# Group 4's keys and queries of a packed attention loaded as whole rows and transposed by PE and ACT; one line of the planner's transfer times and the issue order made anew

## The chip, the cores and the metric

The kernel runs on one core of a Trainium2 chip. The metric is the device time of one execution in microseconds (us). A core has five engines with their own instruction queues: PE (matrix products, with PEld loading its weights), DVE (vector work), ACT (activations and copies), POOL and SP. SP here only issues DMA transfers, which run on the core's 16 DMA engines.

## The reference

A packed attention in two stages feeds a gated feed-forward block. All arrays are float32, except the weights of the block, which come as float64 and are narrowed on the chip.

```python
# batch 8, heads 8, seq 576, head_dim 64, 32 packing queries, d_model 512, d_ff 1024
def _attn_ref(q, k, v, p):
    scale = 1.0 / np.sqrt(q.shape[-1])
    def sm_attn(qq, kk, vv):
        s = scale * np.matmul(qq, kk.transpose(0, 1, 3, 2))
        s = s - np.max(s, axis=-1, keepdims=True)
        a = np.exp(s)
        a = a / (np.sum(a, axis=-1, keepdims=True) + 1e-09)
        return np.matmul(a, vv)
    p_packed = sm_attn(p, k, v)          # 32 rows per head
    return sm_attn(q, p_packed, p_packed)

def _moe_ref(x, w_in, conv_w, w_out):    # x: heads side by side
    h = np.maximum(x @ w_in, 0.0)
    ...                                  # conv_out: 3 taps along the sequence
    gate = 1.0 / (1.0 + np.exp(-conv_out))
    return (h * gate @ w_out)
```

## The kernel before

**Groups.** The 64 pairs of batch and head are worked in 16 groups of four heads, g = 0 to 15; a batch is two groups. For each group the kernel loads the keys and queries (`load_kq`), the values (`load_v`, two transfers) and, for four groups at once, the packing queries (`load_p`). Keys and queries must stand with the head dimension on the partitions, so each is transposed (`head_transpose`). `attention` then has PE multiply packing queries and keys (line 450), DVE take the row maximum (495), ACT take the exponential (499), PE transpose it (525, copied by ACT in 528; from g = 10 on DVE and small transfers do this, 507 to 518), PE multiply with the values (535), ACT divide (546), PE transpose (551) and ACT copy the packed rows (554). The second attention is one more score (450), a transpose on DVE (559), a softmax (563 to 578), a transpose (583) and a split in a high and a low part (587, 589).

**Two layouts of keys and queries.** `by_block(g)` (lines 356 and 357) says which is used. Where it holds, one transfer brings whole rows (line 394: 128 partitions of 1152 numbers), PE transposes them in nine 128x128 pieces (434) and ACT copies them out of PSUM in two pieces of 640 and 512 columns (440). Where it doesn't, four transfers bring 32-number pieces of rows (405), and DVE transposes in one instruction (417). `in_order` and `as_scored` follow the same switch for the order of the columns of the scores. Before, it holds for g below 4.

**The block.** Instead of making the attention's output, the kernel multiplies the packed rows with w_in (`packed_weight`, line 609; high part 621, low part 625 and 629 in batches 0 and 1, and 632 later), and multiplies the second attention's probabilities with that (`ffn1`, line 661: 12 products for each of 8 batches x 8 slices of d_ff). ReLU, the three taps and the gate follow on ACT (673, 677, 687) and DVE (679, 683, 689). `ffn2` splits the result (700, 703) and multiplies it with w_out (752, eight steps of three products for each of 36 tiles of 128 rows), copies (760) and stores (762). w_in and w_out come in eight loads of 1 MB (295); ACT and DVE narrow them (265, 267, 272); w_out is also split (323, 328, 332).

**The order.** Every piece of work is a stream of steps (a Python generator), and the string `ORDER` says which stream makes its next step; each engine gets its instructions in that order and works them strictly so. `Flow` follows the same steps with planned times. These times only decide one thing in the program: where the plan has PE idle, `warm` puts in products that nobody reads (line 244, called fillers below). `SLOW` stretches the planned time of a transfer that begins before a given time. PSUM holds three buffers `big`, one `sm` and one `fo`.

Of the kernel before, what the change touches and what calls it, by code (L numbers as in the profile page):

```python
# [18 lines left out]


ORDER = (
    "0002043m0408043u0304030305060b3l0c06013k050b060c0g0c0c0b060605053q3v3k0e06070e070a3k063v06063k0j060e3v09060j3s0k"
    "0f0j0o060k0e0f3n0k0i0h3r3r060k0d063k0e0m0d3k3r060d0r0e0e0d060e060e060m060e0m0r3t0m0m3t0s0r400e3w0w0s0e0s0n0z0e0e"
    "3t0s0l0e0n060z0z0l0l0e3y170e46460m0q060m0e0u0e0u0l0m460m0e41460p410m170m0e0m0u17480u3x493x480v410v0m0u3x48410m4a"
    "49484a10474849474a3z0m414948413z491f4a49124248470u0u4a4a474b124b0t490u124b0t14433z0u0t0m4a434b0m4c0t4d1f4b4b434c"
    "0u441f4d0x4c4b3z12120u4e18434e3z1a0u4c120m4d4c4g3o6e130u1a154c3z0u131a124c6e450m0u434e4d45126e0u4e434g4f0m456e4g"
    "1a0u1n0m0u124f6e1n451l4d4e4f6e0u454f4d1a4h1c4e4e0u0u4f4g1b0y1k4d451b4i4f4f114j4i7e1n7e4k4i6e1g4h6f4j6e6e4i6f6e4k"
    "4h4k4i4j4i7f161i121a4k4j4i6e1i6f6f121e1a4j4k4l7f1d126f6f6f6f4j4k4l1i6f1o4k6g121s4l1i4l6g4h124l7g4m1a4l6f1a1j4m1q"
    "191j1i1a6f4m4j121i6g1q7g1w6g6h6e4n6g4m6h1q204n1a1v6g1i6g4m1v4l1h6g4m1a4n124m121r1v4n6g6g236f7h1a6g4o121i4n1i4o4p"
    "6h6h4o4p4p1a236h124o7h4o6h4n1q6g4p1a6h6h6h4p6h4o1m4o1a1y4n234p4p1q1i6h1i1q4q282b1y4r6i1r1y6i1y1a1i6i126i6i1q1a2b"  # L30
    "4r6i12241a4q4q1z6i6j1a6i1a4r1i6i6i4s6i2b1p4s6j4s1q4t4u1q4s1i1y1i4t4s264t1t4t1q1z6k1y2g6j2c4u6j1y4u4s261i6j2j4u6j"
    "4s6k6j264u2j4v4t2j1q6j271i4u1u4v226i4u6j266j4t2e1x4w2k6j4t1i4v1q2e1i1q6k4w2e4v2a1i1q6h2f2e4v3p6k6k6k4w1y1i274x26"
    "6k1q6k6l1y4x6l216k6k6k2f4x1q6k4x2m1y4v50266m1q6l6l4w264v1q2r2m6l2h4w6l2m2r506l4x2r6l4y4w1q4y291y6l6l4w501q4y6l6m"
    "4z6m4z262o2n4x1q6m4z2e6m4y6m6m2z1y4x4z6m264y4y4z524z1y4y52524z6l6m251y522s6m34536n535354542e6m2m542e26512u526n6n"
    "6o6n546j6n261y516n532z54526n2z6n6n6n52541y376n516o376p5554553753536m6o262u6o2w552e5630266o6o55266o5635535655266o"
    "6o57552n5756551y56566o2i6p6o1y586p262u6p586q562e596p262d58596p6p6n596p2m6p1y586p6q58576p2m2e6o2u57595a1y5732592m"
    "6q2l1y58586q57266q596q6q3232572m3f2m6q362q6q592e266r6q5b6q262m6r3f2e265a5b6r6r6s6p6r6r5a5c2m6r6s2e5d6r6r5c2e6r5c"
    "5d2m5b5c5c5d5e6r2m6s2e5c6s5e325c5f2u2e5d5e5e6r5d5d383f5e5f2e6s5f5e336s6s6t2v5f6s6s2e6t5k3a2m5d2p2u6s5f5f6s5k5g6t"
    "5e2m3c5g3a2x6t5g2v6t5h2m6t2e6q2m6t2u6t6u2e325k2m6t6u5h2u6t5h6t5f5h5i5h6t3g5h2e5i6u2m5i6u2t2y6u6u5h6u5j333a3a6v5g"
    "6u5j2u6u6u5i5g5i5j326u6v2u3i5j2m5i5j5j5i6v6v6v2m5g5m2u6v6u5m5j5m2u5n6v2u5g325m6v3a6v6w5m6v3d5m3i6w5n5n6v5o5m6w6w"  # L40
    "32313i6w3b6x3i6w5n32325o3a5l5n5o6w3j5l6v5o6w6x32326w6w5o3b325n2u325p6w6x6y5n325l5p3j6x5q6s5o5o6x3a2u5r6x6x5p6x5p"
    "2u5q5q5r6x6x5r6y5p5p3a5q3i6x3e6z5r5p325s2u5q6x325q5s2u5r6y2u6y6y6y3a5q5s5t6z396y2u6y5r5r6y5t6y3a3i5u5t5s6y5t5s3a"
    "325s2u5t325t5s5u325v5t6z326z6z5u6z6w6z3i703i6z703i6z3a6z5v5w5w5v3a5x6z3a5y703a5w5x5w705y5w5w703h5y7070705y5w706y"
    "705x5x713a70715z5z3a5x5y3i64715y703i3i715x3i5x5y5z7172713a5z5z3i3a6071716071603a605z7161717264603i6z60613i723i3a"
    "3i5z726172727271617260727261627372627373626274636261733i73616473743i653i6263736573637363636273736673636674747466"
    "6367676667747474667466687574676872746675676967657568676969767569756a6969756976757575756b6a75776a686a76766a6b6b76"
    "6a7676767675766b76776a6c77786c77776b766b6b7768686c776d6d776c776d7777786c6d6c686d7878786c74786d787878786d79797a79"
    "79797979797a787979787b7a7a7a7a7977797b7a7a7a7a7c7a7b7b7b7b7a7b7b7c7b7b7b7c7c7d7c7c7d7c7c7c7c7d7d7d7d7d7d7d7b7c7d"
    "7d7d7d7d7d7d7i7d7d7c7d7i7d"
)  # L50


# [11 lines left out]
class Flow:  # L64
# [16 lines left out]
    }  # L81
    ISSUE = dict(SP=(465, 1100), POOL=(1050, 1000))
    LATER, LANES = 620, 8
    SLOW = ((4600, 1.28), (5500, 1.7))

    def __init__(self, tokens, warm, busy):
        self.tokens = {k: [(0.0, None)] * n for k, n in tokens.items()}
# [55 lines left out]
    def transfers(self, step, at):  # L143
        issue, delay = self.ISSUE[step.engine]
        for _ in range(step.parts):
# [3 lines left out]
            self.issued += step.engine == "SP"  # L149
            slow = next((x for t, x in self.SLOW if self.data < t), 1.0)  # L150
            self.data = max(self.data, at + delay) + step.ns / step.parts * slow
# [33 lines left out]
def tile_packed_attention_conv_gate(  # L185
# [16 lines left out]
    NG = H // HG  # L202
# [151 lines left out]
    gw = {}  # L354

    def by_block(g):
        return g < NG * 2


    def head(g, i):  # L360
# [2 lines left out]
    def in_order(ap, g):  # L363
        if by_block(g):
            return ap.rearrange("c (r j x) -> c r j x", x=2, j=PR)
        return ap.rearrange("c (j x r) -> c j x r", x=2, r=32)

    def as_scored(ap, g):
        if by_block(g):
            return ap.rearrange("c x (j r) -> c r j x", r=NR)  # L370
        return ap.rearrange("c x (j r) -> c j x r", r=32)
# [12 lines left out]
    def load_kq(g, name, src):  # L384
        b, gg = divmod(g, NG)
        if by_block(g):
            i = g + (NG if name == "q" else 0)
            after = [("kT", i - 3)] if g < NG and i >= 3 else []
            yield Step("SP", 1400, after=after, take=["kq"] * (g >= NG), sets=[(name, g)])
            if g < NG:  # L390
                t = hgt[0].rearrange("r j s -> r (j s)")[:, i % 3 * KQ : (i % 3 + 1) * KQ]
            else:
                t = wk.tile([128, KQ], F32, name=name, tag="kq", bufs=3)
            nc.sync.dma_start(
                out=t, in_=src[b, HG * gg : HG * gg + HG].rearrange("h (r s) d -> (h r) (s d)", r=NR)
            )
            grp[g][name] = t
            return
        yield Step("SP", 4300, take=["kq"], sets=[(name, g)], parts=4)
        t = wk.tile([128, KQ], F32, name=name, tag="kq", bufs=3)  # L400
        t = t[:, : HG * S // 2].rearrange("r (b d) -> r b d", d=32)
        rows = src[b, HG * gg : HG * gg + HG].rearrange("h (j x r) d -> x r (h j) d", x=2, r=32)
        for x in range(2):
            for db in range(2):
                nc.sync.dma_start(
                    out=t[64 * x + 32 * db : 64 * x + 32 * db + 32], in_=rows[x, :, :, 32 * db : 32 * db + 32]
                )
        grp[g][name] = t
# [412 lines left out]
```

## Time and profile before

| | us |
|---|---|
| median of three runs | 407.02 (406.36 to 407.58) |
| the profiled execution | 406.22 |
| its span, first to last instruction | 404.4 |
| PE busy in the span | 395.5 |
| DVE busy | 340.2 |
| ACT busy | 275.2 |

The span is 1.8 us shorter than the execution that it belongs to, and this execution was 0.8 us shorter than the median. In the profile's lines "PE big L434" is PE's instruction of line 434 that writes the tile `big`; `<-` stands between what is written and what is read, or, in the view of waits, between who waited and whom it waited for. An "x5" counts instructions. Some products are recorded as two instructions each: a filler is one of them, so 34 fillers are 68 records.

### The profile page before, as it was taken

How to read it: one execution, taken by the hardware profiler on the slowest of the kernel's cores; microseconds unless marked ns; L12 is line 12 of the kernel's file. 1: busy time of each engine (PE TensorE's matmuls, PEld its weight loads, DVE VectorE, ACT ScalarE, POOL GpSimd, SP SyncE). 2: the span in 40 equal slices, each digit the busy share in tenths (PEclk: the TensorE clock that was granted, in tenths of full speed). 3: DMA queues.
4: the chain of work that ended last, by engine and by line, in shares of the span. 5: the costliest groups of instructions: out<-in, count | busy, mean ns of one | idle time of the engine just before them, and what ended most of it. 6: DMA issues, size and time to landing. Idle time of an engine off the chain costs nothing.

```text
span 404.4 us, 8231 instructions
## 1 busy us (share of the span) xinstructions
PE 395.5 (98%) x3319; PEld 317.6 (79%) x3319; DVE 340.2 (84%) x494; ACT 275.2 (68%) x475; POOL 0.9 (0%) x12
## 2 busy tenths in 40 slices
PE   7899999999999999999999999999999999999996
PEld 6668677787868878888778788788687878887886
DVE  0789999999999999999999999999889886557220
ACT  4889999977668486867566756687666676655121
POOL 0000000000000000000000000000000000000000
PEclk9999999999999999999999999999999999999999
DMA  8999999997947876496563715316001000010211
GB/s 298 366 366 233 293 257 163 137 157 128 134 96 105 129 190 128 88 186 103 107 99 99 151 55 101 129 30 113 28 2 52 28 18 35 26 53 0 78 53 52
DMA packets 140377, 49.19 MB, mean 122 GB/s; under 512 B 121244, under 2 KB 132788, under 8 KB 140340
## 3 DMA queue, kind: packets, MB, share of 16 engines
q1 hardware_dynamic: 140340, 48.67, 53.9%
q8 instruction: 26, 0.43, 0.5%
q14 instruction: 11, 0.09, 0.1%
HBM read 37.25 MB, written 9.44 MB: 115 GB/s over the span
## 4 chain that ended last, share of the span: by engine, by line
PE 74%; DMA 8%; ACT 8%; DVE 5%; SPq 3%; issue 1%; ACTq 0%
PE fo L752 42%; PE big L661 19%; PE sm L752 3%; DMA hgt<-in_moe_w_in_dram 3%; PE big L450 3%; PE big L609 2%; PE sm L535 2%; SPq L515 2%; DMA s<-in_moe_conv_w_dram 2%; DMA v<-in_v_dram 2%; ACT hgt L677 1%; ACT hbuf L673 1%; ACT hgt L687 1%; ACT wo_hi L323 1%; PE big L525 1%
## 5 line engine op out<-in xcount | busy, mean ns | idle before, releaser
L752 PE MATMUL fo<-wo_hi,xhi 128*128 128x512 f32 (+1 forms) x272 | 109.8, 404 | 0.7 <-ACT o L760 0.7
L752 PE MATMUL fo<-wo_hi,xlo 128*128 128x512 f32 (+1 forms) x272 | 106.5, 392 | 0.0
L752 PE MATMUL fo<-wo_lo,xhi 128*128 128x512 f32 (+1 forms) x272 | 106.1, 390 | 0.0
L673 ACT ACTIVATE hbuf<-big 128x576 f32<-128x576 f32 x64 | 41.8, 657 | 32.2 <-PE big L661 32.1
L752 PEld LDWEIGHTS fo<-wo_hi,xhi 128*128 128x128 f32 x272 | 51.2, 188 | 15.7 <-issue 3.0
L679 DVE SCALAR_TENSOR_TENSOR hgt<-hbuf,cw,hgt 128x576 f32<-128x576 f32 x64 | 51.2, 806 | 13.7 <-ACT hgt L677 13.3
L752 PEld LDWEIGHTS fo<-wo_hi,xlo 128*128 128x128 f32 x272 | 51.1, 188 | 12.3
L703 DVE TENSOR_TENSOR xlo<-hgt,xhi 128x1024 fp32r<-128x1024 f32 (+1 forms) x44 | 44.7, 1021 | 16.7 <-ACT xhi L700 16.6
L752 PEld LDWEIGHTS fo<-wo_lo,xhi 128*128 128x128 f32 x272 | 51.1, 188 | 8.5
L661 PE MATMUL big<-a2hi,ghi 128*128 128x288 f32 x256 | 55.8, 299 | 0.1
L687 ACT ACTIVATE hgt<-hgt 128x576 f32<-128x576 f32 x64 | 43.7, 690 | 15.9 <-DVE hgt L683 15.7
L661 PE MATMUL big<-a2hi,glo 128*128 128x288 f32 x256 | 54.4, 294 | 0.0
L661 PE MATMUL big<-a2lo,ghi 128*128 128x288 f32 x256 | 54.2, 293 | 0.0
L683 DVE SCALAR_TENSOR_TENSOR hgt<-hbuf,cw,hgt 128x576 f32<-128x576 f32 x64 | 50.8, 804 | 0.4
L689 DVE SCALAR_TENSOR_TENSOR hgt<-hgt,hbuf 128x576 f32<-128x576 f32 x64 | 47.2, 744 | 4.6 <-ACT hgt L687 4.3
L677 ACT ACTIVATE hgt<-hbuf,cw 128x576 f32<-128x576 f32 x64 | 49.8, 783 | 0.9
L661 PEld LDWEIGHTS big<-a2hi,ghi 128*128 128x128 f32 x256 | 42.9, 188 | 5.9 <-ACT glo L629 1.0
L700 ACT CAST xhi<-hgt 128x1024 fp32r<-128x1024 f32 (+1 forms) x44 | 38.9, 891 | 10.8 <-PE fo L752 6.4
L760 ACT COPY o<-fo 128x512 f32<-128x512 f32 (+1 forms) x34 | 19.6, 578 | 33.3 <-PE fo L752 28.7
L661 PEld LDWEIGHTS big<-a2lo,ghi 128*128 128x128 f32 x256 | 40.9, 188 | 0.0
L661 PEld LDWEIGHTS big<-a2hi,glo 128*128 128x128 f32 x256 | 40.8, 188 | 0.0
L495 DVE TENSOR_REDUCE nm<-big 128x1 f32<-128x576 f32 x16 | 11.9, 746 | 10.6 <-PE big L450 10.6
(91 smaller groups left out, 494.1 us busy)
## 6 DMA issues: line engine op xcount, KB each, us to landing
out_dram<-o SPq DMA_DIRECT2D x35, 256.0 KB, 2.5
v<-in_v_dram SPq DMA_DIRECT2D x16, 512.0 KB, 5.8
k<-in_k_dram SPq DMA_DIRECT2D x48, 144.0 KB, 4.1
q<-in_q_dram SPq DMA_DIRECT2D x48, 144.0 KB, 4.1
hgt<-in_moe_w_in_dram SPq DMA_DIRECT2D x3, 1024.0 KB, 11.2
hgt<-in_moe_w_out_dram SPq DMA_DIRECT2D x3, 1024.0 KB, 6.5
a1T<-stage SPq DMA_DIRECT2D x96, 20.0 KB, 1.8
hgt<-in_k_dram SPq DMA_DIRECT2D x2, 576.0 KB, 5.0
```

The lines of the kernel that those rows point to most:

```text
L450: nc.tensor.matmul(out=o.rearrange("c (j r) -> c j r", r=NR) if by_block(g) else o, lhsT=lhs[r, 32 * i : 32 * i + 32], rhs=rhs[r, :, h, :] ...
L661: nc.tensor.matmul(out=t[:, hf, :SH], lhsT=w[:, gg, js], rhs=x[:, hf * SH : (hf + 1) * SH], start=n == 0, stop=n == 3 * NG - 1,)
L673: nc.scalar.activation(out=h[:, 1 : S + 1].rearrange("c (f s) -> c f s", f=2), in_=t[:, :, :SH], func=AF.Relu, scale=0.5)
L677: nc.scalar.activation(out=d, in_=h[:, 1 : S + 1], func=AF.Copy, scale=cw[:, NJ + j : NJ + j + 1])
L679: nc.vector.scalar_tensor_tensor(out=d, in0=h[:, 0:S], scalar=cw[:, j : j + 1], in1=d, op0=ALU.mult, op1=ALU.add)
L683: nc.vector.scalar_tensor_tensor(out=d, in0=h[:, 2 : S + 2], scalar=cw[:, 2 * NJ + j : 2 * NJ + j + 1], in1=d, op0=ALU.mult, op1=ALU.add)
L687: nc.scalar.activation(out=d, in_=d, func=AF.Tanh)
L689: nc.vector.scalar_tensor_tensor(out=d, in0=d, scalar=1.0, in1=h[:, 1 : S + 1], op0=ALU.add, op1=ALU.mult)
L700: nc.scalar.copy(out=hi[:, js, o], in_=src[:, js])
L703: nc.vector.tensor_tensor(out=lo[:, js, o], in0=src[:, js], in1=hi[:, js, o].bitcast(F32), op=ALU.subtract)
L752: nc.tensor.matmul(out=t[:, : fs.stop - fs.start], lhsT=x[:, c, :], rhs=w[:, c, fs], start=c + i == 0, stop=c == NJ - 1 and i == 2)
L760: nc.scalar.copy(out=o[:, fs], in_=sums_of[m, q][:, : fs.stop - fs.start])
```

## The change

`by_block` takes one group more: g = 4, the first group of batch 2. Its keys and queries come by one transfer each, and PE and ACT transpose them. The planned stretch of transfers is changed, and the order is made anew from the first step to the last; one line of it stands for the table.

```diff
 ORDER = (
-    "0002043m0408043u0304030305060b3l0c06013k050b060c0g0c0c0b060605053q3v3k0e06070e070a3k063v06063k0j060e3v09060j3s0k"
...
+    "3m030300043n3k030b0404020b043l0b080505010j0606060j0c0j3k3k053k070c06060c0c0607060r0e063s05060g0e063t3t0r0e0k0r0k"
...
-    SLOW = ((4600, 1.28), (5500, 1.7))
+    SLOW = ((4600, 1.28), (5500, 1.15), (16500, 1.0), (56000, 1.085))
...
     def by_block(g):
-        return g < NG * 2
+        return g < NG * 2 + 1
```

In the program, PE gets 90 transposes at line 434 in place of 72 and 24 fillers in place of 34. ACT gets four copies more at line 440. DVE has 22 transposes at line 417 in place of 24. The other counts stay.

**SP's transfers from the fifth on, up to the values of group 1.** The rows name the buffer and the input; `hgt_76` and `hgt_77` are memory lent to early loads, `stage` a buffer for a weight. Before:

```order
L295 DMA stage<-in_moe_w_in_dram 128x2x1024
L378 DMA v<-in_v_dram 128x4x256
L382 DMA v<-in_v_dram 64x4x64
L339 DMA s_155<-in_moe_conv_w_dram 24x256
L394 DMA k<-in_k_dram 128x1152
L295 DMA hgt_77<-in_moe_w_in_dram 128x2x1024
L394 DMA hgt_76<-in_q_dram 128x1152
L378 DMA v<-in_v_dram 128x4x256
L382 DMA v<-in_v_dram 64x4x64
```

Now:

```order
L394 DMA hgt_76<-in_q_dram 128x1152
L394 DMA hgt_76<-in_k_dram 128x1152
L378 DMA v<-in_v_dram 128x4x256
L382 DMA v<-in_v_dram 64x4x64
L295 DMA hgt_77<-in_moe_w_in_dram 128x2x1024
L394 DMA k<-in_k_dram 128x1152
L394 DMA hgt_76<-in_q_dram 128x1152
L378 DMA v<-in_v_dram 128x4x256
L382 DMA v<-in_v_dram 64x4x64
```

The last three rows of both are the queries (`hgt_76`) and values of group 1. Two loads of w_in stood ahead of them, and one does now. Ahead of these rows stand four transfers: keys, queries, packing queries and keys before; packing queries, keys, packing queries and the taps of the convolution now.

**PE from the keys of group 2 to the second score of group 1.** `idle` is a filler, `hgt_76` in line 434 the queries of group 1, and line 535 the product with that group's values. Before:

```order
L434 MATMUL big<-ident,k 128x128 x4
L244 MATMUL idle<-ident 128x128 x3
L434 MATMUL big<-ident,hgt_76 128x128 x5
L345 MATMUL sm<-ident,cw_raw 128x24
L450 MATMUL big<-kT,pT 32x288 x8
L244 MATMUL idle<-ident 128x128
L434 MATMUL big<-ident,hgt_76 128x128 x4
L535 MATMUL sm<-v,a1T 32x64 x20
L244 MATMUL idle<-ident 128x128
L551 MATMUL sm<-ident,pb 128x128
L244 MATMUL idle<-ident 128x128 x2
L450 MATMUL big<-qT,ppT 32x288 x8
```

Now:

```order
L434 MATMUL big<-ident,k 128x128 x9
L345 MATMUL sm<-ident,cw_raw 128x24
L434 MATMUL big<-ident,hgt_76 128x128 x5
L525 MATMUL big<-ident,a_261 128x128 x5
L450 MATMUL big<-kT,pT 32x288 x8
L434 MATMUL big<-ident,hgt_76 128x128 x4
L535 MATMUL sm<-v,a1T 32x64 x20
L434 MATMUL big<-ident,k 128x128 x5
L551 MATMUL sm<-ident,pb 128x128
L434 MATMUL big<-ident,k 128x128 x4
L450 MATMUL big<-qT,ppT 32x288 x8
```

Seven fillers stood in this stretch, and none does; the nine transposes of group 3's keys (the second `k`) have come in between.

**ACT around the start of the gate's first slice.** `kT` is copied here for group 4, which before had no such step; `hbuf` is the first slice's output. Before:

```order
L629 CAST glo<-big 128x1024
L499 ACTIVATE a_563,sm_564<-big,nm 128x576
L483 COPY pT<-sm 128x2x32 x2
L265 ACTIVATE hgt_77<-hgt_77 128x1024
L673 ACTIVATE hbuf_78<-big 128x576
```

Now:

```order
L629 CAST glo<-big 128x1024
L528 COPY a1T<-big 128x640
L440 COPY kT<-big 128x640
L440 COPY kT<-big 128x512
L483 COPY pT<-sm 128x2x32 x2
L265 ACTIVATE hgt_77<-hgt_77 128x1024
L673 ACTIVATE hbuf_78<-big 128x576
```

The two copies of group 4's keys stand between the low part of the first packed weight and the first slice.

More of the change, by code (lines that the diff above doesn't have):

```diff
@@ L21 @@
 ORDER = (
-    "0002043m0408043u0304030305060b3l0c06013k050b060c0g0c0c0b060605053q3v3k0e06070e070a3k063v06063k0j060e3v09060j3s0k"
[L23 to L46, printed above, removed]
@@ L47 @@
-    "6a7676767675766b76776a6c77786c77776b766b6b7768686c776d6d776c776d7777786c6d6c686d7878786c74786d787878786d79797a79"
-    "79797979797a787979787b7a7a7a7a7977797b7a7a7a7a7c7a7b7b7b7b7a7b7b7c7b7b7b7c7c7d7c7c7d7c7c7c7c7d7d7d7d7d7d7d7b7c7d"
-    "7d7d7d7d7d7d7i7d7d7c7d7i7d"
+    "3m030300043n3k030b0404020b043l0b080505010j0606060j0c0j3k3k053k070c06060c0c0607060r0e063s05060g0e063t3t0r0e0k0r0k"
+    "060k06060a3k090d0f0k3t3k0d0e0o0f0m3q0d0m060e0i0m0e060s060e0e0d0e060h0n0s0z0s0e060s060m0z0m0e3r0e3u0z173r0w0l0e3r"
@@ new lines @@
+    "0l0u0u0e0e0n060e0l463w060e0e0u0m460v0m0u3y0m0l0m0e3v3v0m460m100p170e460u1010100e3v170m3x48480q3x0v49140m3x0m4a48"
+    "491f0m3z12470u48493z484a48120y470m0u0t0t0u404a47494849490u124b3z4a49130t4b47124a18134c4b0t4b120m0u1a4a4b4c0u0x11"
+    "3z4b421c1f4a0u1f413z4c1a11121a4d4b6e123z4112444c41416e4c0u4d1k154e116e4c0u430m434e410u4d4c110u124f1n1b411g1n0u6e"
+    "0m1a430m4d4e0u4d1a4f436e4d0m4g1n1i45454g430u6e1i4g160u4d450u1i1a4e12124g4f4i4f1s4e454f43454e1b4e4i121a1i1a4f454f"
+    "7e121j4j7e4k4i6e6e4j6e1j6e4k1o191i1a1q4j1a4k4i6f4j3o6f6e7f1a4k1d4h1q1v121i4k4i7f6f4h1i1q4j6f4k6g6f1q6f1e1v1a1v6f"
@@ new lines @@
+    "6f4i1r4k4j6f4h4l6g1i1a6f1w4h4l7g6f1a4i1i4m236g4l4m4m231h4j1a4n7g1r6h6g1q6g4n6g4l1y4l124m6h4m1l1a231y121a4l4n1y4n"
+    "3p1q1z124l6e4m4q6g2b6g1q4n6g7h4m4n4o126g4o6g4p4o6h124n204p4p6h241z6h2g1t7h4o124p6h4o2b286h6h1y2b4o4p6h4q6h6f1a4p"
+    "6g1m4o1y4p6h124q6i1y261y6i1i4r1a2j1q6i266i1a1a6i1i4r6i264s6i4s4t1q6i6j1p1i4t4t4s264r1i4u2c6i6j271i4t4s6i2e4u1q27"
+    "6i4t1u4s1i6k4t266j6j2k6j2e6j224t1i1i6j4s4v4s6j6k4u2e4u4v2j1x4v2j2f1q1q1i6i6j2e6j1i4w6j4u6k6k4v4w4w1y1y1i4u6k6k6k"
+    "6l6k6k6k4u1q4w1q4v4x6j6k4w212m1q4w264x6l4w4x1q2i1y6m504v1y6l2m502m4x4v4y266l4x4x6l2f6l2r1y1i6m1q6l4y6l6l2r6l6k4z"
@@ new lines @@
+    "1y1q1q2n294y1y504y4y2o6l6m4z2r1q6m6m4z4y6m6m1q264z4y4x4z6m262m525225534z2z6m522e4z532s2h6m2e6n6n6h5251531y266m2u"
+    "2e6o266n2a2q526n6n2e516n546o2d6n6n6n5252531y6n6m542m542e55266n53556l5154532z6o546o2z26546o6p6o531y541y5655262u6o"
+    "552p6o2626345537565756561y556p6o6o2e55572l2n6o1y2e572m2u5a6p582w6p26566p56576o6q586p262v6p6p2u576p576p58566q6p57"
+    "2m5a591y265a6q6n596q372u6q6q5859372659585958596q6q58596q2m2m6q2v6q306r5b2m2u5b326r266r6r6r6p6r6s2m2m2e2m6r3c323f"
+    "5c326s2u6r5d2t5c6r5c6r6r6r5e6s5b2e383f6s5d5d5c2e6t5c6s325d6s5d6s6s6s6s5c6t332m5c5e335d2m2e5f6s5d5e6q6t5e2m6u5e5f"
@@ new lines @@
+    "6s5e5g2e2x5g6u3a5k325e5h5g2e5f5g3f3a5k6t6t3a6t5f2e6t365g6t5h5f5h6t3a5f5f6t2u6t5h5i5g2m2e2m6u5h6u5i2e2e2y5h5h5k6u"
+    "6u6v2u5i6u6t5i3g6v2m5i6u6u5j5j6u5j6u5l322u2m3i6v5g3d6v2m5i2u2u3i5m2u5m3i5i6v5m6v3b2u5j5n5j6v6v5j6v313a5j5l356w32"
+    "5m3b6v2u6v3j5o6w6w6w5m2u5n6w6w5n5o326w6w5n6x2u6w6v5n5n5n326w6u5p5l6x5o5o2u6w5o6x5m5p325m5u323a6y325p5p6x5q2u6x3j"
+    "6x5o5p5q6x6x6x3i6x5p6y5o5u5p325q5q3i3a6w325q5q5r5s6x6y326y6y32392u3a6z6y5q5s5r5r2u6y6z5s6x325r325s5t6y5r6y3e5s6y"
+    "5t3a5r325v3i3a5t5s6y325t5t6z6z5s5t3i3i5r6z5t6z705u3a326z6z6z6z703a6z5w5x5w705w6z5w5y705x5x3a705w705w5v5x3a705w5x"
@@ new lines @@
+    "3h5y5v5z705y3i705z5y3a3i5x64715z705y5x705y603i6064713a715z3i717071715y606171723i5z6071715z6071603i6y72716062645z"
+    "3a623a3i7172623a72727372733a7272726162726372733i73613i3i747361633a7363733i3i737374613i61736165737472636374656663"
+    "74636662666262757466667474747474757667686668667568686867687569657567757468697575677675696975756a6a76766967676967"
+    "76766a766b766a7776736a6b69766c6a6b77766a6d6c77766d6b6d6b77776d776d776c77776b6c786c6d786c6d7777787878787778786b78"
+    "6c787979797a79797a797979787978797a797a7a7a7a7a7b7a7a7b757b7c7a7b7b7a7b7b7b7b797c7b7c7b7d7c7c7c7c7c7c7d7c7d7d7d7c"
@@ L50 @@
+    "7d7b7d7d7d7d7d7i7c7d7d7d7d7d7d7i7d7d7d"
 )
```

## The prediction

> **What bounds the kernel now.** I read the windows of 10 us first, because an average over the span mixes stages. The columns are PE, PEld, DVE, ACT and POOL busy (with instructions), the granted clock, the DMA engines' busy share and GB/s.
>
> ```profile
> 0.00:10.00 10.00, 7.93 (x59) 6.98 (x59) 0.76 (x1) 4.54 (x9) 0.90 (x12) 1.00 0.82 297
> 10.00:20.00 10.00, 8.34 (x117) 6.24 (x117) 7.36 (x15) 9.06 (x21) 0.00 (x0) 1.00 1.06 367
> 20.00:30.00 10.00, 9.50 (x136) 6.38 (x134) 8.87 (x18) 8.09 (x20) 0.00 (x0) 1.00 1.05 363
> 30.00:40.00 10.00, 9.87 (x139) 8.32 (x131) 9.70 (x16) 9.78 (x18) 0.00 (x0) 1.00 0.96 232
> 40.00:50.00 10.00, 9.68 (x112) 6.14 (x110) 10.00 (x15) 9.86 (x18) 0.00 (x0) 1.00 1.05 307
> 50.00:60.00 10.00, 10.00 (x118) 7.44 (x118) 9.71 (x15) 10.00 (x17) 0.00 (x0) 1.00 1.01 264
> 60.00:70.00 10.00, 10.00 (x70) 6.88 (x67) 9.89 (x17) 10.00 (x18) 0.00 (x0) 1.00 1.11 160
> ```
>
> From 50 us on PE is never idle in these rows, so what PE hasn't done by then it must still do: time is won or lost in the ramp before. There the DMA engines are full from 10 us on, and ACT is full from 30 us on. The waits name what was late: first PE's own over the whole span, then ACT's of the first 30 us (us in total, times, longest).
>
> ```profile
> PE big L434 <- ACT s L569: 1.4, 1, 1.4
> PE big L434 <- DMA q<-in_q_dram: 0.3, 1, 0.3
> PE sm L535 <- DMA v<-in_v_dram: 0.3, 1, 0.3
> ```
>
> ```profile
> ACT kT L440 <- PE big L434: 4.3, 2, 3.9
> ACT pb L546 <- PE sm L535: 1.5, 1, 1.5
> ACT qT L440 <- PE big L434: 0.4, 1, 0.4
> ```
>
> The 1.4 us is the transposes of group 1's queries, whose operand is a transfer (line 394); the exponential named there touches neither it nor its buffer, so I take the load for the true releaser. ACT's 1.5 us is the same story one step on: it divides group 1's product, which had to wait for the values. Last, the chain that ended last (start, us, what) shows who held PE once the loads no longer did:
>
> ```profile
> 49.24 0.72 ACT a L499 x2
> 49.96 0.66 ACT hgt L677
> ...
> 56.91 0.95 ACT wo_hi L323
> ...
> 64.32 0.91 ACT wo_lo L332
> ...
> 71.53 0.92 ACT glo L629
> 72.50 5.06 PE big L661 x36
> ...
> 81.94 0.83 PE sm L535 x40
> ...
> 84.36 1.59 PE big L661 x12
> ...
> 136.63 0.65 PE big L450 x16
> ...
> 147.47 0.86 PE big L609 x16
> ...
> 184.54 0.69 ACT hgt L687
> ```
>
> From 49 to 72 us the chain runs mostly through ACT, and the low part of batch 1's packed weight (71.53) is the last step that releases PE. After that it is PE almost throughout.
>
> **The change part by part.** Single prices come from the timeline:
>
> ```profile
> 4.58 2.18 PE L434 MATMUL big<-ident,hgt 128*128 128x128 f32 x9 [0.56 <-DMA hgt<-in_k_dram]
> ...
> 10.14 1.17 ACT L440 COPY kT<-big 128x640 f32<-128x640 f32 x2
> ...
> 14.41 0.61 PE L244 MATMUL idle<-ident 128*128 128x128 f32 x4
> ...
> 15.77 0.71 PE L434 MATMUL big<-ident,k 128*128 128x128 f32 x5
> ...
> 16.90 0.60 PE L434 MATMUL big<-ident,k 128*128 128x128 f32 x4
> ```
>
> ```profile
> 56.47 1.02 PE L328 MATMUL big<-tmp,ident 128*128 128x512 f32 x2
> ...
> 58.74 0.72 PE L450 MATMUL big<-kT,pT 64*32 64x288 f32 x16
> 59.38 0.84 PE L535 MATMUL sm<-v,a1T 128*32 128x64 f32 x36
> ```
>
> *PE's bill.* Four transposes take 0.60 us and five 0.71, so one more costs 0.11; 18 cost 2.0 us. Four records of fillers take 0.61, like four transposes, so a filler (two records) costs 0.22; ten fewer give 2.2 back. Together -0.2 us, all on PE. The Trainium skill, "TensorE: Matmul & The Clock Gate", section "Back-to-back issue gap", gives about 56 ns between warm products of 128 columns; by that the transposes would cost 1.0 us and the bill would be 1.0 us lower. The rows above show twice that, and I keep them.
>
> *DVE's bill.* Two transposes fall away:
>
> ```profile
> L417 DVE STREAM_TRANSPOSE kT<-k 128x1152 f32<-128x1152 f32 x12 | 16.4, 1366 | 0.2 <-PE big L450 0.2
> ```
>
> That is 2.7 us of DVE, but DVE is the releaser in none of PE's own rows, so I count nothing; the cover is PE's own backlog from 50 us on.
>
> *ACT's bill.* A pair of copies takes 1.17 us, so four add 2.3 us in a stretch where ACT is full. What counts is what stands ahead of the step that last held PE. There the new order has four copies (2.3), one exponential (0.72) and two small copies (0.2 by a guess of 0.1 each) more, and one instruction less of each of lines 677 (0.66), 687 (0.69), 323 (0.95) and 332 (0.91): +3.2 and -3.2, so nothing. PE pays for that exchange later. Behind the products released there it has one packed weight (0.86) and one tile of w_out (56.47 to 58.74, 2.3) more still to do, and two scores (2 x 0.65) and one product with values (0.83) less: +1.0 us.
>
> *The loads.* Sizes (KB each, then us to landing):
>
> ```profile
> v<-in_v_dram SPq DMA_DIRECT2D x16, 512.0 KB, 5.8
> k<-in_k_dram SPq DMA_DIRECT2D x2, 576.0 KB, 10.8
> stage<-in_moe_w_in_dram SPq DMA_DIRECT2D x1, 1024.0 KB, 8.3
> v<-in_v_dram SPq DMA_DIRECT2D x16, 64.0 KB, 5.3
> p<-in_p_dram SPq DMA_DIRECT2D x4, 128.0 KB, 6.1
> ```
>
> Ahead of group 1's queries and values stands 1024 KB of w_in less and 128 KB of packing queries more: 896 KB, or 0.92 MB, which at 366 GB/s (10 to 30 us) is 2.5 us. Ahead of group 2's queries it is 1024 KB, 2.9 us. Group 4's keys and queries take 0.59 MB each; at the 160 GB/s of 60 to 70 us, where such pieces were loaded with the engines full, that is 3.7 us, and as rows at 366 GB/s 1.6. So 4.2 us of transfer go, about half of it before 50 us.
>
> *What comes of it.* ACT's waits for group 1's values (1.5) and queries (0.4) should go, since both land 2.5 us sooner. Two preparations of packing queries and a copy now stand ahead of ACT's first key copy, where it idled for 3.9 us; I take 0.5 us for them. That is 2.4 us. Next late are group 2's queries: 2.9 us sooner, against an ACT that comes 2.4 us sooner and has a little less in front of them. I take 2.4, with 1.5 as the low end (the values alone) and 0 as the end at which something else holds ACT. The sum at the step that last held PE: 1.0 - 2.4 = -1.4 us. PE's -0.2 is not added, since there PE waits for ACT. From the median of 407.02 that is **405.6 us**; from the profiled execution's 406.22, 404.8, with the same 1.8 us outside the span.
>
> **The rivals.** *ACT gains nothing* (the copies stand where it is full, and another wait takes the place of the values'): the +1.0 us stays alone, 408.0 us. For it: ACT is full from 30 to 70 us, and I have given it 2.3 us more; against it: the two waits are plain rows, and their loads are moved up by more than they lasted.
>
> *PE alone decides* (ACT is nowhere the last): PE's bill of -0.2 and its three waits (1.4 + 0.3 + 0.3), all for loads that now come earlier: -2.2 us, 404.8 us. Against it speaks the chain from 49 to 72 us.
>
> *A load runs late, and it is slower.* PE's product with group 4's values stood at 59.38; two slices of line 661 (2 x 1.59) and one tile of w_out (2.3) no longer stand ahead of it, so with the 1.4 us it is wanted at about 52.5. The new order has 15,600 KB (16.0 MB) to bring up to these values. Before, 15.7 MB had come by 50 us (the GB/s of five rows), and 16.0 by 51.3; less 2.1 us for the keys of group 4, 49.2. That leaves 1 to 3 us. If the loads behind 30 us (10.3 MB by then) all run at the 232 GB/s of 30 to 40 us, the values land at 54.7: PE stands for 2.2 us, and the loads behind them, two tiles of w_out and group 6's keys, for which DVE waits in its queue, are as late. That is 2.2 to 4 us on the forecast; at 3.2 it gives 408.8 us. It decides from a landing at 52.5 on.
>
> *The clock drops.* At 4.58 us nine transposes took 2.18 us, twice the later price, so PE ran slow in its first 5 us; ten fewer fillers could bring that back in a thin stretch of the ramp. Another 5 us at half speed cost 2.6, so 408.2 us. Against it: a wait of 1.4 us at 18 us changed nothing, though the granted clock reads 1.00 in the slow stretch too and so can't tell. The Trainium skill, "TensorE: Matmul & The Clock Gate", section "Part 4: PE-mode transpose", says that transposes don't count as activity that keeps the clock up, which speaks against trading fillers for them; the 0.60 and 0.71 us above are warm all the same, between other products.
>
> That the change doesn't do what it says is excluded: the row loads and the copies of group 4 stand in the order.
>
> **How the numbers follow.** A difference of 0.3%, 1.2 us, is about what a measurement of this kernel can tell from none: faster is under 405.8, slower over 408.2. The forecast gets 0.50; its own range is 404.6 to 406.5 (ACT's gain between 1.5 and 3.4 us, 3.4 if the order also removes the small waits that I left), so I put 0.37 of it faster and 0.13 the same. PE alone: 0.13, faster. ACT gains nothing: 0.22, the same. Late load: 0.11, and the clock: 0.04, slower. That makes 0.50, 0.35 and 0.15. The range of 403.8 to 408.4 reaches from a little under PE alone, since the prices of the bill may be 1 us off, to over the ACT rival; it leaves out most of the late load.
>
> **What would show it.** Right: PE idle in the windows from 10 to 50 us falls from 2.6 us to under 1.5, the wait of PE at line 434 and that of ACT at 546 are gone, ACT is still full from 30 to 70 us, and the low part of batch 1's packed weight is made at about 69 us. Wrong: that step is no earlier than 71 us; or PE waits at line 535 for `v` behind 50 us; or transposes at 0.22 us come again behind 10 us; or DVE, with 2.7 us less to do, turns out to have held PE, and the gain is larger than 2.2 us.

## The result: slower, and the profile after

| | before | after |
|---|---|---|
| median, us | 406.66 (406.22 to 407.58, six runs) | 410.07 (409.35 to 411.15, six runs) |
| ratio, 95% interval | | 1.0093 (1.0078 to 1.0107) |
| the profiled execution, us | 406.22 | 410.09 |
| its span, us | 404.4 | 408.3 |

The kernel became 3.4 us slower by the medians and 3.8 by the ratio, where 1.4 us faster was forecast. The windows of the kernel after have the columns of those of before:

```profile
0.00:10.00 10.00, 6.50 (x26) 5.32 (x26) 0.00 (x0) 3.77 (x9) 0.91 (x12) 1.00 0.81 246
10.00:20.00 10.00, 9.57 (x132) 6.46 (x132) 4.88 (x10) 8.21 (x20) 0.00 (x0) 1.00 1.06 359
20.00:30.00 10.00, 9.61 (x154) 6.62 (x152) 9.55 (x18) 9.09 (x21) 0.00 (x0) 1.00 1.02 372
30.00:40.00 10.00, 9.99 (x128) 8.15 (x114) 9.96 (x18) 10.00 (x19) 0.00 (x0) 1.00 1.02 350
40.00:50.00 10.00, 9.61 (x126) 7.68 (x125) 9.72 (x16) 10.00 (x19) 0.00 (x0) 1.00 0.89 210
50.00:60.00 10.00, 9.98 (x121) 7.53 (x121) 10.00 (x17) 10.00 (x19) 0.00 (x0) 1.00 0.97 246
60.00:70.00 10.00, 10.00 (x70) 6.20 (x70) 9.99 (x17) 10.00 (x19) 0.00 (x0) 1.00 0.95 232
70.00:80.00 10.00, 9.18 (x97) 6.44 (x97) 9.53 (x16) 9.51 (x15) 0.00 (x0) 1.00 0.91 172
```

From 10 to 50 us PE idles 1.2 us, where it was 2.6 before: the ramp is fuller, as forecast. But the first 10 us hold 1.4 us less of PE's work (6.50 for 7.93) and none of DVE's, DVE does 4.88 for 7.36 in the next ten, and PE idles 0.8 us between 70 and 80. PE's waits over the whole span name the places, and ACT's of the first 30 us show what has become of the waits of before:

```profile
...
PE fo L752 <- ACT o L760: 1.2, 2, 0.7
PE big L434 <- DMA hgt<-in_q_dram: 1.0, 1, 1.0
PE big L434 <- DMA hgt<-in_k_dram: 0.7, 1, 0.7
PE big L328 <- ACT wo_lo L332: 0.7, 1, 0.7
```

```profile
ACT kT L440 <- PE big L434: 2.6, 2, 2.4
ACT qT L440 <- PE big L434: 1.8, 2, 1.6
ACT a L499 <- DVE nm L495: 1.4, 2, 1.1
ACT pm L474 <- DMA p<-in_p_dram: 1.0, 1, 1.0
...
ACT pb L546 <- PE sm L535: 0.4, 1, 0.4
```

ACT's 1.5 us for group 1's values are gone (the 0.4 left is group 0's division, at 15.7 us), so those loads do come in time. But ACT waits longer for the transposed queries (1.8 us for 0.4), for the first maximum (1.4 for 0.8) and, which is new, for packing queries (1.0). New is also a wait of PE for the queries of group 0, the first group of all. The timeline of before around the first score, and then that of after (start, us, engine, line, what, and in brackets the idle time with its releaser):

```profile
6.55 0.65 PE L244 MATMUL idle<-ident 128*128 128x128 f32 x4
...
7.15 0.71 PE L434 MATMUL big<-ident,hgt 128*128 128x128 f32 x5
7.79 0.71 PE L450 MATMUL big<-kT,pT 64*32 64x288 f32 x16
...
8.61 0.76 DVE L495 TENSOR_REDUCE nm<-big 128x1 f32<-128x576 f32 x1 [8.61 <-PE big L450]
```

```profile
5.44 2.18 PE L434 MATMUL big<-ident,hgt 128*128 128x128 f32 x9 [0.72 <-DMA hgt<-in_k_dram]
...
8.87 1.33 PE L434 MATMUL big<-ident,hgt 128*128 128x128 f32 x5 [1.03 <-DMA hgt<-in_q_dram]
10.13 1.21 PE L450 MATMUL big<-kT,pT 64*32 64x288 f32 x16
...
11.45 0.76 DVE L495 TENSOR_REDUCE nm<-big 128x1 f32<-128x576 f32 x1 [11.45 <-PE big L450]
...
12.07 1.23 PE L434 MATMUL big<-ident,hgt 128*128 128x128 f32 x9
```

The first score needs keys and packing queries, not queries. But five transposes of the queries stand ahead of it in PE's queue in both kernels, and the queries are now the fifth transfer, not the second. So PE waits for them, and what follows runs slow (1.33 us for 0.71, 1.21 for 0.71), at the price of the nine transposes that take 2.18 us. Products have their later price again from 6.55 us before (four records of fillers in 0.65 us) and from about 12 us now (nine transposes in 1.23). DVE's first maximum comes 2.8 us later; by the runs in the last section about 1.9 of these are usual. The chain that ended last leads back to that transfer:

```profile
2.83 6.00 DMA hgt<-in_q_dram
...
8.87 1.33 PE big L434 x5
10.20 1.14 PE big L450 x16
...
29.94 0.74 ACT a L499 x2
...
35.78 0.18 ACT kT L440
...
44.70 0.59 ACT qT L440
...
72.12 0.90 ACT glo L629
...
74.63 0.92 ACT wo_lo L332
...
75.60 2.45 PE big L328 x6
```

From 30 to 75 us it is ACT almost without a break, with group 4's copies (35.78, 44.70) in it. The low part of batch 1's packed weight stands at 72.12, where the forecast had about 69.

### The profile page after: what moved, and what is told of

Same layout as the page of the kernel before. It is cut to its first block, busy times and chain, and to the rows that moved or that the text cites. A ratio compares the mean times of both kernels' runs of the same rounds, so it can differ in the third digit from the quotient of the medians.

```text
span 408.3 us, 8224 instructions
## 1 busy us (share of the span) xinstructions
PE 397.8 (97%) x3317; PEld 317.4 (78%) x3317; DVE 339.1 (83%) x492; ACT 278.0 (68%) x479; POOL 0.9 (0%) x12
## 4 chain that ended last, share of the span: by engine, by line
PE 71%; ACT 13%; DVE 7%; SPq 4%; DMA 3%; issue 1%; DVEq 0%; ACTq 0%
PE fo L752 39%; PE big L661 18%; PE sm L752 3%; PE big L450 3%; PE big L609 2%; SPq L515 2%; PE sm L535 2%; DMA hgt<-in_q_dram 1%; PE big L434 1%; ACT hgt L677 1%; ACT hbuf L673 1%; DVE hgt L679 1%; ACT hgt L265 1%; SPq L405 1%; ACT hgt L687 1%
```

## The experiments

The theories were these: the late start is passed on to the end; the copies on a full ACT are what costs; some other part of the new order loses it. The 95% intervals are those of each kernel's ratio to the kernel before, run on the same chip.

| kernel | median, us | ratio to before |
|---|---|---|
| after | 410.07 | 1.0093 (1.0078 to 1.0107) |
| after, start as before | 408.56 | 1.0041 (1.0026 to 1.0057) |
| after, first score ahead of the queries | 409.35 | 1.0066 (1.0043 to 1.0089) |
| before, new layout alone | 410.83 | 1.0101 (1.0084 to 1.0118) |
| after, old layout | 416.03 | 1.0218 (1.0197 to 1.0240) |
| before, late start | 407.07 | 1.0020 (1.0007 to 1.0032) |
| after, 18 transposes more | 411.31 | 1.0124 (1.0095 to 1.0152) |
| after, four ACT copies more | 412.06 | 1.0137 (1.0120 to 1.0154) |
| before, few fillers | 407.20 | 1.0026 (1.0012 to 1.0040) |
| after, one load put back | 411.97 | 1.0149 (1.0127 to 1.0171) |
| after, copies on DVE | 413.42 | 1.0168 (1.0149 to 1.0188) |
| after, two casts swapped | 409.60 | 1.0083 (1.0065 to 1.0102) |
| after, start as before and casts swapped | 408.63 | 1.0056 (1.0037 to 1.0075) |
| before, that load later | 407.31 | 1.0014 (1.0003 to 1.0025) |
| before, 2.7 us more on DVE | 408.33 | 1.0041 (1.0029 to 1.0053) |
| before, 18 transposes more | 408.18 | 1.0036 (1.0025 to 1.0048) |
| before, four ACT copies more | 408.66 | 1.0048 (1.0029 to 1.0068) |

Where the text below gives a difference in us, it is the difference of the ratios times 406.5, unless it says medians. A ratio's interval is 0.4 to 1.2 us wide on either side, so a difference of two kernels is known to about 0.6 to 1.3 us. `Flow` plans each order anew, so a new order can also have another number of fillers; the kernel before has 34 and the kernel after 24.

**The start put back.** In ORDER two characters are a step; 00, 02 and 08 load the keys and queries of group 0 and the keys of group 1, `3m` and `3n` the packing queries, `3k` the taps.

```diff
-    "3m030300043n3k030b0404020b043l0b080505010j060606...
+    "0002043m0408040304030305060b3l0b0b053n3k010j0606...
```

> The kernel after, with only the start of the order (its first 24 steps) as it was before: keys and queries of group 0 are loaded first and second, the packing queries third; everything behind these steps keeps the new order, and group 4 stays on PE and ACT. Theory 1 (the start): DVE's first row maximum came at 11.45 us instead of 8.61, and this passes on to the end, as DVE and ACT have next to no idle time from 20 to 70 us. Then the first maximum is back near 8.6 and the time falls by 2 to 2.8 us, to 407.3 to 408.1. Theory 2 (the copies): group 4's four copies, 2.3 us, on an ACT that is full to 70 us hold PE, and the start is absorbed: the time stays within 0.8 us of 410.1. Theory 3 (the rest of the new order loses it): it stays as well, at 409.3 to 410.5.

The first score and the first maximum now:

```profile
8.69 0.72 PE L450 MATMUL big<-kT,pT 64*32 64x288 f32 x16
...
9.52 0.76 DVE L495 TENSOR_REDUCE nm<-big 128x1 f32<-128x576 f32 x1 [9.52 <-PE big L450]
```

The maximum comes 1.9 us earlier than in the kernel after, and the time falls by 2.1 us (1.5 by the medians). So the start is a cause, and not the only one: 1.7 us over before remain. The plan puts 33 fillers in this kernel, nine more than in the kernel after, so the run doesn't part the order of the loads from these; the run with few fillers below lets them be worth a few tenths.

**The first score ahead of the queries.** The loads stay as they are in the kernel after; the two steps `05`, five transposes of group 0's queries and their copy, go behind the first score; the other four stood there already.

```diff
-    "...3l0b080505010j060606...
+    "...3l0b08010j0606050506...
```

> The kernel after, with the loads as they are now (queries of group 0 fifth), but the nine PE transposes of these queries put behind the first score in PE's queue instead of ahead of it. This takes from the first score the wait for the queries (1.0 us) and the cold transposes of five blocks (0.6 us), and leaves the keys' landing at 5.40 us. Theory 1: the first maximum comes 1.2 to 1.6 us earlier, at 9.9 to 10.3, and the time falls to 408.5 to 408.9. Theories 2 and 3: within 0.8 us of 410.1.

The first maximum came at 10.60 us. Measured were 409.35, a gain of 1.1 us whose interval overlaps that of the kernel after. It points the same way, but doesn't settle anything by itself.

**The layout alone.** Group 4 is taken by `by_block`, in the order of before; each of its two transposing steps is written four times.

```diff
-        return g < NG * 2
+        return g < NG * 2 + 1
```

> The kernel before, its order and planned transfer times kept, with group 4's keys and queries as whole rows, transposed by PE and copied by ACT at the places of the order where DVE transposed them. Theory 1: the copies cost what the prediction counted, ACT 2.3 us in a queue that holds PE's last step less what is gained, so 406.5 to 408. Theory 2: all of the loss is here, 409 to 410.5. Theory 3: the layout costs little, 406.5 to 407.5.

It costs 4.1 us, so layout plus start would be more than the whole loss. Here some of it is bad placing. In its timeline the queries of group 4 are transposed at 75 us, where DVE used to do it:

```profile
75.34 0.71 PE L434 MATMUL big<-ident,q 128*128 128x128 f32 x5
76.09 0.69 ACT L440 COPY qT<-big 128x640 f32<-128x640 f32 x1 [0.99 <-PE big L434]
...
76.83 0.66 PE L434 MATMUL big<-ident,q 128*128 128x128 f32 x4 [0.78 <-ACT qT L440]
...
78.17 0.53 PE L661 MATMUL big<-a2hi,ghi 128*128 128x288 f32 x2 [0.68 <-ACT qT L440]
```

PE waits 1.5 us for the copies there, and its window from 70 to 80 us holds 8.46 us of work, where before had 9.92.

**The old layout in the new order.** `by_block` is set back, and of each group of four steps only the first is kept.

> The kernel after, its order and planned transfer times kept, with group 4's keys and queries transposed by DVE as before (four transfers each, no copies on ACT). Theory 1: the late start stays, so 409 to 410.5, though the copies are gone. Theory 2: without the copies ACT is 2.3 us ahead, and the time falls to 407 to 408. Theory 3: 409 to 410.5 as in theory 1, with PE's gaps at 44, 72 to 78 and 201 us still there.

At 416.03 us it fits none of the three. In its waits ACT stands 2.8 us for a load of w_in; group 4's keys, now in pieces, are ahead of one in SP's queue:

```profile
ACT hgt L265 <- DMA hgt<-in_moe_w_in_dram: 2.8, 1, 2.8
```

Its plan also puts in 60 fillers, 36 more than in the kernel after, and PE is busy for 402.8 us of its span, where it is 397.8 in the kernel after. That kernel has a loss of its own, and says nothing of the copies.

**The late start alone, in the kernel before.**

```diff
-    "0002043m0408043u0304030305060b3l0c06013k...
+    "3m030300043k0304040204083u05060b3l0c0601...
```

> The kernel before (group 4 on DVE, order and planned times of before) with only the first loads put as they are now: packing queries, keys of group 0, taps of the convolution, queries of group 0. Putting the start back in the kernel after took 1.5 us off (408.56 against 410.07). Theory 1 (the late first score is passed on to the end): the first maximum comes 1.5 to 2.5 us later than 8.61 us and the time rises by as much, to 408 to 409. Theory 2 (the start only costs because the new order has no slack behind it): the order of before has 1.9 us of idle ACT between 20 and 30 us and absorbs it, 406.5 to 407.2.

The first maximum came at 11.42 us, yet the time rose by only 0.8 us: the second theory. ACT's waits behind 9 us show what took it up:

```profile
ACT a L499 <- DVE nm L495: 1.3, 1, 1.3
ACT pb L546 <- PE sm L535: 1.0, 2, 0.8
ACT qT L440 <- PE big L434: 0.9, 1, 0.9
```

The wait for group 1's values was 1.5 us and is 0.8 at the longest; PE's 1.4 us for that group's queries is gone. A late start and an early load draw on the same idle time.

**Each engine's share doubled in the kernel after.** Group 4's transposes, and in another kernel its copies, are made twice.

```diff
-            for j in range(lo, hi):
+            for j in [j for _ in range(1 + (g == 4)) for j in range(lo, hi)]:
```

```diff
-            nc.scalar.copy(out=o[:, lo * 128 : hi * 128], in_=t[:, : (hi - lo) * 128])
+            for _ in range(1 + (g == 4)):
+                nc.scalar.copy(out=o[:, lo * 128 : hi * 128], in_=t[:, : (hi - lo) * 128])
```

> The kernel after, with group 4's 18 transposes each done twice on PE: 18 transposes of 0.11 us more, 2.0 us of PE's time, none on ACT, fillers as they were. Theory P (PE is bound wherever these stand, and its bill goes whole into the time): 412.1. Theory A (what counts are ACT's copies): at most 0.7 us more, 410 to 410.8.

> The kernel after, with group 4's four copies each done twice on ACT: 2.3 us of ACT's time more, none on PE. Theory A (ACT's queue is full from 24 to 72 us and sets when PE goes on): 412 to 412.5. Theory P: at most 0.7 us more, 410 to 410.8. Both at once, with 2 us in each of the two runs, would say that PE and ACT hold each other in turn in this stretch.

2.0 us more on PE cost 1.3, and 2.3 us more on ACT cost 1.8. ACT's cost is clear of the noise. PE's is not, since its interval overlaps that of the kernel after. It points to what the second text calls holding each other in turn, and the same two additions to the kernel before, further below, show it more clearly.

**Few fillers in the kernel before.**

```diff
-        while self.matmuls(at, self.FILL_NS, self.FILL_COLS, False) + self.MARGIN <= until:
+        while at < 10000 and self.matmuls(at, self.FILL_NS, self.FILL_COLS, False) + self.MARGIN <= until:
```

> The kernel before without its 27 fillers behind the first 10 us of the plan, and nothing else changed. They are 5.9 us of PE's time by 0.22 us each. If a filler takes PE's time, as the sum of the prediction had it for the 10 that go, the time falls by up to 5.9 us, to 400.6 to 404.5. If fillers only fill waits of PE that are there anyway, it stays within 0.6 us of 406.6, and the 18 new transposes had no fillers to pay for them. If they keep PE fast, it rises.

The time rose by 1.1 us, so fillers give nothing back when they go. The profiled execution, at 408.75 us, shows the last case of the text. Its timeline of PE and then its windows:

```profile
17.47 0.60 PE L434 MATMUL big<-ident,k 128*128 128x128 f32 x4
20.01 0.74 PE L434 MATMUL big<-ident,hgt 128*128 128x128 f32 x5 [1.94 <-ACT s L569]
...
21.49 1.03 PE L434 MATMUL big<-ident,hgt 128*128 128x128 f32 x4
...
25.23 1.22 PE L450 MATMUL big<-qT,ppT 64*32 64x288 f32 x16 [0.35 <-ACT ppT L554]
```

```profile
18.00:20.00 2.00, 0.07 (x1) 0.02 (x1) 2.00 (x3) 2.00 (x4) 0.00 (x0) 1.00 1.12 323
20.00:21.00 1.00, 0.99 (x14) 0.80 (x22) 1.00 (x2) 0.71 (x2) 0.00 (x0) 1.00 1.03 400
21.00:22.00 1.00, 1.00 (x19) 0.54 (x8) 0.90 (x4) 0.82 (x3) 0.00 (x0) 0.81 1.02 387
22.00:23.00 1.00, 1.00 (x25) 0.67 (x27) 1.00 (x3) 0.00 (x0) 0.00 (x0) 0.50 1.03 418
...
26.00:28.00 2.00, 2.00 (x16) 1.63 (x9) 1.42 (x2) 0.95 (x1) 0.00 (x0) 0.50 1.12 328
28.00:30.00 2.00, 1.99 (x16) 1.75 (x15) 2.00 (x4) 2.00 (x6) 0.00 (x0) 0.89 1.02 386
```

Left alone, PE stands for 1.9 us at 18 us, and from 21 to 28 us the granted clock goes down to 0.50: four transposes take 1.03 us for 0.60, a score 1.22 for 0.72. But only four of the twelve executions lost clock in this way: their mean granted clock is 0.987 to 0.995, and they took 407.46 to 409.47 us. The other eight, at 0.999 or 1.000, have a median of 407.0 us, which is still in the range of the second case, where fillers only fill waits.

**One load put back in the kernel after.** The step that loads the second piece of w_in stands ahead of the queries of group 1 again; every filler is kept at its place by number.

> The kernel after, every engine's order and every filler as they are, with only the second load of w_in (1 MB) put back ahead of the queries and values of group 1 in SP's queue, where it stood before. These two then land about 2.9 us later, as before. Theory G (the earlier loads were the gain that was forecast, 2.4 us, and it is there, hidden under larger losses): the time rises by 1.5 to 2.9 us, to 411.6 to 413. Theory N (there was no such gain, since the late start already delays ACT by more than the loads did): within 0.7 us of 410.1.

Measured 2.3 us over the kernel after, and PE's waits (its line numbers are 3 higher) show the values late:

```profile
PE sm L538 <- DMA v<-in_v_dram: 0.9, 1, 0.9
```

In that order the early loads are worth what theory G says.

**The copies on DVE.**

```diff
-            nc.scalar.copy(out=o[:, lo * 128 : hi * 128], in_=t[:, : (hi - lo) * 128])
+            copy = nc.vector.tensor_copy if g == 4 else nc.scalar.copy
+            copy(out=o[:, lo * 128 : hi * 128], in_=t[:, : (hi - lo) * 128])
```

> The kernel after, with group 4's four copies out of PSUM made by DVE instead of ACT; nothing else changes. Theory A (ACT holds PE, DVE has 2.7 us less to do than before and holds nobody): ACT is 2.3 us freer and the time falls by 1.5 to 2.3, to 407.8 to 408.6. Theory B (DVE, full from 46 us as well, holds PE as much as ACT does, and what it lost with the two transposes is worth something): within 0.8 us of 410.1.

It cost 3.0 us more, so both theories fall: DVE, the engine that released nobody in PE's waits of before, is dearer than ACT here.

**Two casts swapped, alone and with the old start.** In ACT's queue the low part of a piece of w_out (line 332) goes ahead of the next high part (323).

> The kernel after, with two neighbouring casts of ACT swapped: the one that makes the low part of a piece of w_out and frees the PSUM buffer on which PE waits at 75.6 us now stands ahead of the one that makes the next high part. PE's wait of 0.7 us there (0.8 us of idle PE between 70 and 80 us) should go. If PE is bound from here on, the time falls by 0.5 to 0.8 us, to 409.3 to 409.6; if ACT only hands the wait on, it stays within 0.3.

> The old start in the kernel after (408.56 alone) and the swap of the two casts together. If the two costs lie one behind the other, they add: 407.8 to 408.1. If the earlier start already lets ACT come in time, 408.6.

PE's wait at line 328 is gone from the first kernel's trace, and its window from 70 to 80 us has 9.63 for 9.18:

```profile
70.00:80.00 10.00, 9.63 (x98) 6.60 (x98) 9.96 (x16) 9.82 (x15) 0.00 (x0) 1.00 0.93 165
```

But the intervals overlap in both pairs (409.60 against 410.07, 408.63 against 408.56), so what this wait is worth isn't settled: by the ratios the swap gains 0.4 us in the first pair and loses 0.6 in the second.

**The early load alone, in the kernel before.** The second piece of w_in goes behind the values of group 1, and its casts on ACT and DVE go down to where it lands.

> The kernel before with the one part of the change that the runs so far show as a gain: the second load of w_in (1 MB) goes behind the queries and values of group 1 in SP's queue, and the casts of that piece on ACT and DVE go down their queues to where it now lands; group 4 stays on DVE, the start stays. Putting that load back cost the kernel after 1.9 us. Theory G1 (the gain belongs to the loads, whatever the rest of the order): the time falls by 1.2 to 2 us, to 404.4 to 405.2, below both kernels. Theory G2 (the gain exists only with an order that uses it): within 0.7 us of 406.4.

No gain: 0.6 us slower. PE's 1.4 us for group 1's queries are gone, and its longest wait behind 9 us is now the one for group 2's queries, which was 0.3 us in the kernel before:

```profile
PE big L434 <- DMA q<-in_q_dram: 1.0, 1, 1.0
```

**Each engine's share doubled in the kernel before.** DVE's two transposes of group 4 are made twice; in two more kernels the 18 PE transposes and the four ACT copies of group 3 (as in the diffs above, with g == 3).

```diff
-            nc.vector.transpose(out=o, in_=src.rearrange("r b d -> r (b d)"))
+            for _ in range(1 + (g == 4)):
+                nc.vector.transpose(out=o, in_=src.rearrange("r b d -> r (b d)"))
```

> The kernel before with group 4's two DVE transposes each done twice: 2.7 us of DVE's time more, nothing else changed. The prediction counted the 2.7 us that DVE loses as nothing. If that is right, the same 2.7 us added cost nothing as well: 406 to 407. If DVE holds PE through the ramp, as its four copies did in the kernel after (413.42), the time rises by 2 to 2.7, to 408.4 to 409.1, and taking them away was a gain that something else ate.

> The kernel before with group 3's 18 transposes each done twice on PE: 2.0 us of PE's time at 26 to 50 us, before any change of the order. In the kernel after the same addition at group 4 cost 1.2 us. If PE has room in the ramp of before (1.2 us of idle and 17 fillers between 10 and 30 us), 406.4 to 407.2; if not, 407.6 to 408.4.

> The kernel before with group 3's four copies each done twice on ACT: 2.3 us of ACT's time. In the kernel after the same addition at group 4 cost 2 us. If ACT's idle time of before (2.9 us from 10 to 30 us) hides it, 406.4 to 407.2; if ACT holds PE from 30 us on whatever comes, 408.2 to 408.7. With both additions dear, the layout has no cheap place in this order, and its 4.3 us are PE's and ACT's bills added up.

| added in the ramp of before | us of work | us of time |
|---|---|---|
| PE | 2.0 | 1.5 |
| ACT | 2.3 | 2.0 |
| DVE | 2.7 | 1.7 |

All three are paid, and by these values none in full, though ACT's interval (1.2 to 2.8 us) reaches the full price. If taking work away gives back what adding it costs, the layout's bill is 1.5 + 2.0 - 1.7 = 1.8 us, give or take 1. That the saving on DVE is worth what the addition costs is an assumption, and PE and ACT were loaded at group 3, not 4; the sum agrees with the 1.7 us that the kernel with the old start still loses.

## Why the prediction was wrong

**The sum.** The forecast was +1.0 - 2.4 = -1.4 us. Measured by the ratio were +3.8: 2.1 for the start, and 1.7 for all the rest, which the doublings put at 1.8 for the layout's bills, so that nothing of the forecast gain is left. The profiles also give both terms at the forecast's own mark, the end of the low part of batch 1's packed weight (line 629), as differences to before in us:

| | forecast | after | after, start as before |
|---|---|---|---|
| that step ends | -2.4 | +0.6 (73.0 for 72.4) | -0.7 (71.7) |
| from there to the end of the span | +1.0 | +3.3 (335.3 for 332.0) | +2.5 (334.5) |
| together | -1.4 | +3.9 | +1.8 |

So both terms failed. For the first row a single profile is good to about 1 us: the kernel with the two casts swapped, which is the same up to there, ends this step at 74.1, and the profile of before began early, as the last section shows. The second row holds in every profile: 331.4 to 332.3 us in the seven kernels with the layout of before and, but for single moves, its order; 333.9 to 335.5 in the nine with the new layout and, but for such moves, the new order.

**The step that failed first** is the start: "Two preparations of packing queries and a copy now stand ahead of ACT's first key copy, where it idled for 3.9 us; I take 0.5 us for them." The new order was seen there, and only its use of an idle ACT was priced. That the packing queries' load pushes the keys back, that the queries of group 0 go from second to fifth, and that PE, which works strictly in order, has their transposes ahead of the first score, was not. In place of -0.5 stand +2.1, some tenths of which may belong to the nine fillers. ACT's idle time up to the step of line 629, which the forecast had 2.4 us shorter, is 8.9 us for 8.7: the waits for group 1 went, and those for packing queries, queries and the first maximum took their place.

**The work behind the step.** The +1.0 counted the exchanged pieces rightly: behind the step PE has 16 products of line 609 and six of line 328 more, and 32 of line 450 and 40 of line 535 less. But PE's busy time there grew by 1.9 us (329.6 for 327.7), and its idle time by 1.4 (5.7 for 4.2), of which 0.9 are waits for ACT at lines 328 and 661. What makes the busy time grow by 0.9 more than the forecast stays open.

**The bills.** PE's -0.2 rested on ten fillers giving 2.2 us back. Fillers stand where PE waits anyway, and the kernel without most of them is slower, so what is left is the price of 18 transposes, 1.5 in the kernel before. (The aside that products at 56 ns would lower the bill by 1.0 us halves the transposes alone; the fillers, two such products each, would halve too.) DVE's 2.7 us were counted at nothing because DVE released nobody in PE's waits; adding as much costs 1.7. ACT's "+3.2 and -3.2, so nothing" weighed which ACT work stands ahead of one step; four copies on that engine cost 2.0 in the kernel before and 1.8 in the kernel after. The common error is the last step, "PE's -0.2 is not added, since there PE waits for ACT": it took one engine for the bound of the ramp, when additions on each of three engines with next to no idle time get through for the most part. How the 1.7 us divide between the layout and the rest of the new order stays open, since the two runs that part them each have a loss of their own.

**The loads.** Here the mechanism was right: the waits named are gone, PE's idle time from 10 to 50 us fell to 1.2 as foreseen, and putting one load back costs 2.3 us. But the 1.9 us counted for them are not a gain on the kernel before. Alone they gave none there, since PE then waits for group 2's queries (1.0 us); and in the new order they come together with the late start, which in the kernel before used up the same waits.

**The rivals.** "ACT gains nothing" (408.0) was right that ACT's gain doesn't reach the end, but it too left out the start and the bills. "A load runs late" (408.8) was nearest in size, and named the right kind of event at the wrong place: not the values of group 4 at 52 us, behind which nothing waited at line 535 for `v`, but the first queries at 8.8 us. "The clock drops" has its half of truth there: the slow price lasts to about 12 us instead of 6.5, and PE's transposes and its score at 8.87 and 10.13 us lost 1.1 us by it. No run parts this from the late queries.

**The signs.** The low part of batch 1's packed weight came at 72.12 us, behind the 71 us set as the mark for wrong, and that was the sign to trust. The idle time of PE was not: it fell, while the time rose.

## What to carry to other kernels

Where three engines are each over 95% busy, price an added instruction on any of them at most of its length (here 0.6 to 0.9), whoever is named in the waits; that a removed one gives as much back was assumed here, not shown. Where a forecast has a mark in the middle, read both sides of it from the trace afterwards: here the sum was 3.0 us off ahead of the mark and 2.3 behind it. When an order is made anew, follow the first transfers, and what stands behind them in each in-order queue, up to the first result, before anything in the middle. Work that only fills waits pays for nothing when it goes, and early loads and a late start use the same idle time once.

## What the runs showed of the hardware

Without most fillers, a 1.9 us stand of PE in a ramp that was thin anyway (6.21 us of work from 10 to 20 us) was followed by a granted clock of 0.50 for some 6 us. The Trainium skill, "TensorE: Matmul & The Clock Gate", section "Part 1: The HAM clock gate", says that PE falls to half its clock after about one idle window of 3.4 us; the 0.50 agrees, and the stand that came before it here was shorter than that. It doesn't come every time: four of that kernel's twelve executions have a mean granted clock below 0.999, and so do 8 of the 84 executions of the kernel before that were run beside the experiments; these eight, at 0.996 to 0.998, took 407.27 to 408.18 us, where the medians were 406.25 to 406.52. In the first 10 us of the kernel after, the same column reads 1.00 while nine transposes take 2.18 us, so there the slow price shows in the durations alone.

The start is not the same in each execution: in six kernels that share all first loads with the kernel before, DVE's first maximum came between 9.15 and 10.27 us, and in the profile of before at 8.61. In the eight kernels with the new start and the queries ahead of the first score it came between 11.03 and 11.76 us. The 2.8 us between the two profiles are some 0.9 more than is usual.
